# Bringing the first pair's keys and queries in as 256-byte rows and turning them on TensorE

## The chip, the cores and the metric

The kernel runs on one core of one Trainium2 chip. The metric is the device time of one execution in microseconds (us), lower is better. Durations of single instructions are given in us or ns from one profiled execution. The engines are TensorE (PE, its weight loads are listed apart as PEld), VectorE (DVE), ScalarE (ACT), GpSimd (POOL) and SyncE (SP), which here only issues transfers; ACT issues a few as well.

## The reference, cut to what matters

Attention with a threshold, and then a feed-forward block with ELU on its output:

```python
# q, k, v: (8, 8, 576, 64) fp32; tau: a scalar; w_in: (512, 2048), w_out: (2048, 512)
scores = (1 / sqrt(64)) * q @ k.transpose(0, 1, 3, 2)
thresh = max(scores, axis=-1) - tau
scores = where(scores >= thresh, scores, -1e9)
attn = exp(scores - max(scores, axis=-1))
attn = attn / (sum(attn, axis=-1) + 1e-9)
x = (attn @ v).transpose(0, 2, 1, 3).reshape(4608, 512)
h = x @ w_in
g = where(h > 0, h, exp(min(h, 0)) - 1)
out = g @ w_out
```

## The kernel before, in words

The 64 heads are worked in 32 pairs, two heads of one batch side by side: head 0 of a pair in partitions 0 to 63, head 1 in 64 to 127. Of the 576 positions of a head, 512 (MAIN, NC = 4 blocks of P = 128) make full steps, and the last 64 (TAIL) of both heads make a fifth step. A step is a tile of 128 queries against all 576 keys of both heads: scores on TensorE (`scores`, L673), the maximum on VectorE (`max_of`, L730), threshold or pivot (`bound_of`, `pivot_of`), exponential on ScalarE, mask and sum, normalisation, a turn of the weights (L792 with copies at L808, in the opening) and the product with the values (L925, L930). When the first batches are done, the feed-forward matmuls are woven in, and from then on TensorE works on them between the steps.

The scores need queries and keys with the 64 numbers of a head along the partitions, `qT` of 128 x 576 and `kT` of 128 x (64 + 576). In memory a position is a row of 64 fp32 numbers, 256 bytes. `load` brings a pair in so that VectorE's transpose, which turns blocks of 32 x 32, gives the wanted layout: every row is cut into two pieces of 32 numbers (128 bytes), which go to different groups of 32 partitions, one DMA for each group. `prep_q` and `prep_k` are those transposes. In `kT` the first 64 columns hold, for head 1, a copy of the last 64 keys (`copy_k`, on GpSimd), so that both heads can use halves of 288 keys that start at different columns. For pair 0 `prep_q` turns the first 256 queries alone; the rest follow later (`load_rest_of_q`, `rest_of_q`).

The order of the instructions is written out by hand: `manual_schedule`, with tasks that have a time of their own (`task`, sorted at the end of `early_tasks`) and a table of offsets, MOVED. Each engine runs its instructions in that order and waits where the data isn't there. The first task is `start`, which loads pair 0, keeps TensorE busy with 22 transposes of the identity (`idle(22)`), turns queries and keys, and works out from tau the constants of the thresholds (`read_tau`, six small VectorE instructions, L435 to L440). The tasks after it load pair 1 (which takes over the buffers `qm` and `km` of pair 0), the values, and the rest of the queries. Step 0 works head by head (HEADS_APART): all scores of head 0, then those of head 1.

Matmul outputs lie in PSUM. Up to step LATE there are two pools: `psum["t"]` with two buffers for turns and value products, and `psum["s"]` with three buffers of two banks for scores. `room_for` keeps the handed-out order of the first.

The Exp of `keep` in `start` loads ScalarE's table ahead of its first use.

Of the kernel before, what the change touches and what calls it, by code (L numbers as in the profile page):

```python
# [10 lines left out]
FP32 = mybir.dt.float32  # L11
# [357 lines left out]
def kernel(  # L369
# [10 lines left out]
    nc = tc.nc  # L380
    PSUM = bass.MemoryType.PSUM
    P = 128
    B, H, S, D = q.shape
    DM, DF = moe_w_in.shape
    NC = S // P
    MAIN = NC * P
    TAIL = S - MAIN
    HALF = S // 2
    T = 32
    NT = P // T  # L390
# [11 lines left out]
    const = ctx.enter_context(tc.tile_pool(name="const", bufs=1))  # L402
# [7 lines left out]
    raw = attention.enter_context(tc.tile_pool(name="raw", bufs=1, side="right"))  # L410
# [6 lines left out]
    wstage = early.enter_context(tc.tile_pool(name="wstage", bufs=2))  # L417
    wpool = [wstage]
    banks = ExitStack()
    psum = {"t": banks.enter_context(tc.tile_pool(name="ps_t", bufs=2, space=PSUM))}  # L420

    first = ExitStack()
    psum["s"] = first.enter_context(tc.tile_pool(name="ps_s0", bufs=3, space=PSUM))

    ident = wstage.tile([P, P], FP32, name="ident", bufs=1)
    make_identity(nc, ident)
    idents = [ident]
# [2 lines left out]
    tau_sb = const.tile([P, 1], FP32, name="tau_sb")  # L430
# [15 lines left out]
    def w_in_at(j, f, n):  # L446
        return w_in_sb[f // QF][:, j, f % QF : f % QF + n]
# [4 lines left out]

    xtail = dram.tile([KJ, P, B * TAIL], FP32, name="xtail", bufs=1)

    NQD, NVD = 2, 2
    qds = [const.tile([P, P], FP32, name=f"qd{i}") for i in range(NQD)]
    vds = [const.tile([P, P], FP32, name=f"vd{i}") for i in range(NVD)]
    vds_first = [wstage.tile([P, P], FP32, name=f"vf{i}", bufs=1) for i in range(NVD)]
    for t in qds + vds_first + vds:
        nc.gpsimd.memset(t, 0.0)  # L460


# [1 line left out]
    pieces = [(moe_w_in, w_in_at(j, n, WN), j, n) for n in range(0, DF, WN) for j in range(KJ)]  # L464
# [56 lines left out]
    raws, pairs, firsts = {}, {}, {}  # L521


    def load(pr, parts=("qm", "km", "v"), shared=False, queue=nc.sync, pieces=tuple((i, d) for i in range(2) for d in range(2)),
             js=slice(0, S // T)):
        b, j = divmod(pr, NPAIR)
        tiles = raws.setdefault(pr, {})
        for name, src in (("qm", q), ("km", k), ("qr", q)):
            if name not in parts:
                continue  # L530
            if name not in tiles:
                tiles[name] = raw.tile([P, S // T, T], FP32, name="qm" if shared else name)
            m = tiles[name]
            if pr in QK_PE:
                if "ends" not in tiles:
                    tiles["ends"] = wstage.tile([TAIL, 2, 2, D], FP32, name="ends", bufs=1)
                both, blocks = src[b, 2 * j : 2 * j + 2], blocks_of(pr, name[0])
                for i in range(2):
                    queue.dma_start(blocks[:, :, i], both[i, :MAIN].rearrange("(c p) d -> p c d", p=P))
                queue.dma_start(tiles["ends"][:, int(name == "km")], both[:, MAIN:].rearrange("i p d -> p i d"))  # L540
                continue
            for i, d in pieces:
                r = (2 * i + d) * T
                queue.dma_start(
                    m[r : r + T, js if name != "qr" else slice(0, S // T - js.start)],
                    src[b, 2 * j + i].rearrange("(j t) d -> t j d", t=T)[:, js, d * T : (d + 1) * T],
                )
        if "v" in parts:
            load_v(pr)
# [12 lines left out]
    def room_q(pr):  # L562
        if pr < 2:
            both = wstage.tile([P, 2 * S + TAIL], FP32, name="x", bufs=2)
            qT, firsts[pr] = both[:, :S], both[:, S:]
        else:
            qT = qkp.tile([P, S], FP32, name="qT")
        pairs[pr] = [qT, None, qds[pr % NQD]]
        return qT

    def room_k(pr):
        kT = pairs[pr][1] = firsts[pr] if pr < 2 else qkp.tile([P, TAIL + S], FP32, name="kT")
        return kT

    def prep_q(pr):
        qT, n = room_q(pr), S if pr else 2 * P
        nc.vector.transpose(qT[:, :n], raws[pr]["qm"].rearrange("p j d -> p (j d)")[:, :n])
# [8 lines left out]
    def prep_k(pr):  # L586
        kT = room_k(pr)
        km = raws[pr]["km"].rearrange("p j d -> p (j d)")
        for c0, c1 in ((0, HALF), (HALF, S)) if pr == 0 else ((0, S),):
            nc.vector.transpose(kT[:, TAIL + c0 : TAIL + c1], km[:, c0:c1])  # L590


    def blocks_of(pr, name):
        return raws[pr][name + "m"].rearrange("p j d -> p (j d)")[:, :MAIN].rearrange("p (c i d) -> p c i d", i=2, c=NC)
# [32 lines left out]
    def copy_k(pr):  # L627
        kT = pairs[pr][1]
        nc.gpsimd.tensor_copy(kT[D:, :TAIL], kT[D:, S:])
# [18 lines left out]
    def vectors(pr):  # L648
        st = {x: small.tile([P, 2], FP32, name=x) for x in ("mx", "th", "su", "rs")}
        if not pr:  # L650
            st["nb"] = wstage.tile([P, 2], FP32, name="nb", bufs=4)
        step_no[0] += 1
        st["sm"] = totals[:, step_no[0] % 6]
        return st


    def scores(pr, i, hs):
        qT, kT, qd = pairs[pr]
        if hs[0] == 0:
            open_steps[pr, i] = vectors(pr)  # L660
        st = open_steps[pr, i]
        if "f" in psum and not apart:
            both = psum["s"].tile([P, 2, 2, 512], FP32, name="sc")
            scs = {h: both[:, h] for h in hs}
        else:
            scs = {h: psum["s"].tile([P, 2, 512], FP32, name="sc") for h in hs}
        halves = [(a, h) for a in range(2) for h in hs]
        if (pr, i) in HEADS_APART:
            halves.sort(key=lambda x: x[1])
        for a, h in halves:  # L670
            k0 = a * HALF + (0 if h else TAIL)
            r, qs = (slice(h * D, (h + 1) * D), qT[:, i * P : (i + 1) * P]) if i < NC else (slice(0, P), qd)
            nc.tensor.matmul(scs[h][:, a, :HALF], qs[r], kT[r, k0 : k0 + HALF], start=True, stop=True)  # L673
        if len(hs) == 2 and "f" in psum and not apart:
            st["both"] = both
        for h in hs:
            st[h] = scs[h]
# [617 lines left out]
    def task(x, t, key, f, *needed):  # L1295
        each = "_".join(map(str, x)) if isinstance(x, tuple) else x
        made[x] = [t + (MOVED.get(key, 0.0) if key else 0.0) + MOVED.get(each, 0.0), len(made), f, needed, False]
# [10 lines left out]
    def early_tasks():  # L1308
# [10 lines left out]
        def idle(n):  # L1319
            room_for("t", lambda: None)  # L1320
            rt = psum["t"].tile([P, NC, P], FP32, name="rt", tag="rt")
            for _ in range(n):
                transpose(rt[:, 0], ident)

        def start():
            load(0, ("qm",), js=slice(0, 2 * NT))
            load(0, ("km",), queue=nc.scalar, pieces=((0, 0), (0, 1), (1, 0)))
            load(0, ("km",), pieces=((1, 1),))
            nc.scalar.activation(keep, keep, AF.Exp)
            nc.sync.dma_start(tau_sb, tau.to_broadcast([P, 1]))  # L1330
            idle(22)
            prep_q(0)
            prep_k(0)
            read_tau()
            copy_k(0)

        def load_rest_of_q():
            raws[0]["qr"] = wstage.tile([P, S // T - 2 * NT, T], FP32, name="qr", bufs=1)
# [32 lines left out]
        turned = {}  # L1371
        for pr in range(1, NPAIR + 6):
            old = ("sc", number[pr - 2, NC]) if pr > 1 else None
            own = pr < NPAIR
            for x, name in enumerate("qk"):
                n = 2 * pr - 2 + x if own else number[pr - 1, 2 + x]
                k, late_ = kind(n), n >= LATE
# [30 lines left out]
            for x, name in enumerate("qk"):  # L1408
                n = 2 * pr - 1 + x if own else number[pr - 1, 3 + x]
                late_ = n >= LATE  # L1410
                task(("load", name, pr + 1), begin[n] + (7.0 if late_ else -1.0 if own else 4.6), f"l{name}{kind(n)}",
                     lambda pr=pr, name=name: load(pr + 1, (name + "m",)), ("prep", name, pr), ("last", pr) if pr in QK_PE else None)
            if pr > 1:
                n = 2 * pr - 3 if own else number[pr - 1, 3]
# [5 lines left out]
        for i, (n, x) in enumerate(slots):  # L1420
            late_, k, t = n >= LATE, f"{kind(n)}{x}", begin[n]
# [43 lines left out]
        for u in range(NU):  # L1465
            n = 26 + 3 * u // 2 if u < NU - 2 else SWITCH + u - NU + 2
# [3 lines left out]
        for n in range(MIDDLE):  # L1470
            pr, i = steps[n]
# [4 lines left out]
            t, k, hs, late_ = begin[n], kind(n), heads_of(i), n >= LATE  # L1476
# [3 lines left out]
            if n == LATE:  # L1480
                task("switch", t, None, switch, *rooms)
            rooms += [("exp" if (n, h) in MASK_ACT else "mask", n, h) for h in hs]
            at_ = (lambda a, b, c=0: t + c) if last_ else (lambda a, b, c=0: t + b) if late_ else (lambda a, b, c=0: t + a)
            task(("sc", n), t + 0.2 if late_ else t - 2.6 if i in (2, NC) else t - 2.0, f"sc{k}", lambda pr=pr, i=i, hs=hs: scores(pr, i, hs), ("prep", "q", pr),
                 ("prep", "k", pr), ("scale", pr) if pr else None, ("copy", "k", pr), ("copy", "q", pr) if i == NC else None,
                 ("sc", n - 1) if n else None, "rest" if (pr, i) == (0, 2) else None, *two)
            for h in hs:
# [127 lines left out]
    with tc.manual_schedule():  # L1615
# [31 lines left out]
        ends = []  # L1647
# [226 lines left out]
        queue = deque()  # L1874
# [212 lines left out]
        for pr in range(JOINED, NP + 2):  # L2087
            t = clock[0]
            b = pr // NPAIR
# [93 lines left out]
        for f in range(EARLY_IN + 1, NFT):  # L2183
            t = max(begin + 0.4 + 2.73 * (f - EARLY_IN), start_of[g7, f] - LEAD)
# [78 lines left out]
        for f in range(NFT):  # L2263
            split_weights(begin + 22.0 + 3.9 * f if f < OUT_EARLY else start_f(middle, f) - 9.0, ("out", f), w_out_of(f),
                          lambda f=f: out_done(f))
            for g, t0 in ((g7, middle), (g8, end)):
                t = start_f(t0, f) - (11.5 if f < EDGE else 6.0) + 3.2 * f * (f < EDGE)
# [84 lines left out]
```

## Time and profile before

| what | value |
|---|---|
| median of 3 runs | 1259.23 us (1258.12 to 1259.68) |
| the profiled execution | 1259.32 us |
| its span, first to last instruction | 1257.5 us |
| PE busy in 0 to 32 us, 32 to 64 us, 64 to 96 us | 27.20, 30.20, 32.00 us |
| first score instruction on PE | 6.23 us |
| DMA busy share in 0 to 32 us, mean rate | 0.71, 136 GB/s |

The profile is of one execution. The share of busy time is an average over stages with different limits, so the opening has to be read by itself, instruction by instruction. A line of the timeline gives the start, the length, the engine, the line of the kernel, the operation, what it writes and reads, the shape, how many instructions were merged into it, and in brackets how long the engine had been idle and what ended the wait. "L792 PE MATMUL rt<-ident" is a transpose on TensorE. A matmul's listed length contains its way through the array, so instructions overlap and the pace of a run is its length, less one tail, by their number.

### The profile page before, as it was taken

How to read it: one execution, taken by the hardware profiler on the slowest of the kernel's cores; microseconds unless marked ns; L12 is line 12 of the kernel's file. 1: busy time of each engine (PE TensorE's matmuls, PEld its weight loads, DVE VectorE, ACT ScalarE, POOL GpSimd, SP SyncE). 2: the span in 40 equal slices, each digit the busy share in tenths (PEclk: the TensorE clock that was granted, in tenths of full speed). 3: DMA queues.
4: the chain of work that ended last, by engine and by line, in shares of the span. 5: the costliest groups of instructions: out<-in, count | busy, mean ns of one | idle time of the engine just before them, and what ended most of it. 6: DMA issues, size and time to landing. Idle time of an engine off the chain costs nothing.

```text
span 1257.5 us, 21116 instructions
## 1 busy us (share of the span) xinstructions
PE 1243.9 (99%) x6598; PEld 957.0 (76%) x6598; DVE 1040.3 (83%) x2199; ACT 635.2 (51%) x1331; POOL 727.1 (58%) x1061
## 2 busy tenths in 40 slices
PE   8999999999999999999999999999999999999998
PEld 6676576467878787888778787878788887788886
DVE  7888778789798988898889879898889876776983
ACT  7989776664352526253534435252625353465330
POOL 4778655687475847666576747584766655122000
PEclk9999999999999999999999999999999999999999
DMA  7557688998889898998989998999889885000001
GB/s 134 151 177 177 177 244 234 260 248 216 239 239 266 245 240 224 241 263 228 252 206 253 237 231 231 256 257 240 228 238 262 221 241 175 20 1 1 1 34 34
DMA packets 325551, 245.74 MB, mean 195 GB/s; under 512 B 209216, under 2 KB 289984, under 8 KB 325440
## 3 DMA queue, kind: packets, MB, share of 16 engines
q1 hardware_dynamic: 323264, 243.65, 72.2%
q8 instruction: 52, 0.85, 0.3%
q10 hardware_dynamic: 2176, 0.75, 0.2%
q14 instruction: 59, 0.48, 0.1%
HBM read 154.53 MB, written 89.78 MB: 194 GB/s over the span
## 4 chain that ended last, share of the span: by engine, by line
PE 90%; DVE 3%; DMA 2%; ACT 2%; issue 1%; SPq 1%; POOL 1%; DVEq 0%; ACTq 0%; POOLq 0%
PE f L1678 23%; PE f L1818 22%; PE sc L977 8%; PE sc L1050 7%; PE f L2278 7%; PE f L2203 5%; PE f L1102 4%; PE sc L673 3%; PE f L1154 3%; PE f L2216 2%; PE pv L930 2%; PE rt L792 1%; PE sc L1042 1%; PE sc L1037 1%; DMA there<-x 1%
## 5 line engine op out<-in xcount | busy, mean ns | idle before, releaser
L984 DVE TENSOR_REDUCE mx<-sc 128x1 f32<-128x576 f32 x207 | 148.3, 750 | 28.5 <-PE sc L977 24.6
L726 POOL TENSOR_SCALAR w<-w,rs 128x576 f32<-128x576 f32 x144 | 115.8, 813 | 70.0 <-DVE rs L789 69.8
L1004 ACT ACTIVATE w<-sc,mx 128x576 f32<-128x576 f32 x113 | 81.5, 740 | 116.0 <-DVE mx L984 98.7
L868 DVE STREAM_TRANSPOSE x<-w 128x512 f32<-128x512 f32 (+1 forms) x153 | 108.9, 744 | 15.3 <-POOL w L726 11.3
L996 POOL TENSOR_SCALAR th<-mx,ntau 128x2 f32<-128x2 f32 (+1 forms) x114 | 33.8, 297 | 133.3 <-DVE mx L984 133.3
L977 PE MATMUL sc<-kT,qT 64*128 64x448 f32 (+4 forms) x736 | 103.4, 416 | 0.2 <-ACT xs L1066 0.2
L977 PEld LDWEIGHTS sc<-kT,qT 64*128 64x128 f32 x736 | 81.0, 186 | 25.1 <-issue 16.5
L1011 DVE SCALAR_TENSOR_TENSOR w<-sc,th,w 128x576 f32<-128x576 f32 x113 | 88.2, 811 | 9.4 <-ACT w L1004 9.2
L1678 PE MATMUL f<-xt,sw 128*128 128x256 f32 x384 | 93.8, 386 | 1.8 <-DVE g L1700 1.8
L1678 PE MATMUL f<-xt,w_in 128*128 128x256 f32 x384 | 92.2, 382 | 0.0
L1818 PE MATMUL f<-w_out,s 128*128 128x256 f32 x384 | 92.0, 382 | 0.1
L1818 PE MATMUL f<-w_out,g 128*128 128x256 f32 x384 | 92.0, 382 | 0.0
L1678 PE MATMUL f<-x,w_in 128*128 128x256 f32 x384 | 90.9, 379 | 0.0
L1818 PE MATMUL f<-t,s 128*128 128x256 f32 x384 | 90.8, 379 | 0.0
L726 POOL TENSOR_SCALAR e<-e,rs 128x576 f32<-128x576 f32 x91 | 67.1, 741 | 35.6 <-DVE rs L789 34.2
L1678 PEld LDWEIGHTS f<-xt,sw 128*128 128x128 f32 x384 | 69.4, 189 | 18.6 <-issue 4.8
L1678 PEld LDWEIGHTS f<-xt,w_in 128*128 128x128 f32 x384 | 71.7, 190 | 12.7 <-ACT w L1692 2.2
L1818 PEld LDWEIGHTS f<-w_out,g 128*128 128x128 f32 x384 | 72.0, 190 | 12.4 <-issue 3.1
L1818 PEld LDWEIGHTS f<-w_out,s 128*128 128x128 f32 x384 | 71.9, 190 | 12.4 <-issue 2.5
L1678 PEld LDWEIGHTS f<-x,w_in 128*128 128x128 f32 x384 | 72.8, 190 | 10.5 <-ACT s L1692 0.6
L1818 PEld LDWEIGHTS f<-t,s 128*128 128x128 f32 x384 | 72.8, 190 | 10.3 <-POOL s L1765 0.4
L1765 POOL TENSOR_TENSOR s<-g 128x256 f32<-128x256 f32 x96 | 74.9, 785 | 7.9 <-DVE g L1728 7.5
(316 smaller groups left out, 3103.5 us busy)
## 6 DMA issues: line engine op xcount, KB each, us to landing
there<-x SPq DMA_DIRECT2D x444, 144.0 KB, 3.5
wTb<-there SPq DMA_DIRECT2D x58, 576.0 KB, 6.5
wTa<-there SPq DMA_DIRECT2D x53, 576.0 KB, 5.0
sw<-win_sums SPq DMA_DIRECT2D x46, 384.0 KB, 4.9
t<-wout_sums SPq DMA_DIRECT2D x33, 512.0 KB, 6.2
qm<-in_q_dram SPq DMA_DIRECT2D x124, 72.0 KB, 4.9
wst<-in_moe_w_in_dram SPq DMA_DIRECT2D x16, 512.0 KB, 4.4
vm<-in_v_dram SPq DMA_DIRECT2D x64, 128.0 KB, 3.9
```

The costliest lines, as they stand in the source:

```text
L726: nc.gpsimd.tensor_scalar(wv, wv, st["rs"][:, h : h + 1], 1.0, ALU.mult, ALU.mult)
L868: nc.vector.transpose(x[:, :, c0 : c0 + nc_], src.rearrange("p (c g n) -> p g c n", c=nc_, n=T))
L977: on_banks(nc.tensor.matmul(o, qT[r, i * P : (i + 1) * P], kT[r, k0 : k0 + n], start=True, stop=True, skip_group_check=True), o)
L984: on_banks(nc.vector.tensor_reduce(st["mx"][:, h : h + 1], st["sc", h], axis=AX.XY if i == NC else AX.X, op=ALU.max, negate=True), st["sc" ...
L1004: on_banks(nc.scalar.activation(st["e", h], st["sc", h], AF.Exp, bias=st["mx"][:, h : h + 1]), st["sc", h])
L1011: on_banks(nc.vector.scalar_tensor_tensor(st["e", h], st["sc", h], st["th"][:, h : h + 1], st["e", h], ALU.is_ge, ALU.mult, accum_out=st[" ...
L1050: on_banks(nc.tensor.matmul(o, vm[:, h, c], parts[part][:, g0:g1, h * (NC + 1) + c], start=False, stop=(c == NC - 1), skip_group_check=Tru ...
L1678: nc.tensor.matmul(loc["banks"][place], left[:, j], right[:, j], start=(begins and j == 0), stop=(j == 1), skip_group_check=True)
L1765: engine.tensor_tensor(o, x, y, op)
L1818: nc.tensor.matmul(place(m), lhs, rhs, start=(begins and v == 0), stop=(v == RU - 1), skip_group_check=True)
L2203: nc.tensor.matmul(o, w.rearrange("p (j f) -> p j f", j=KJ)[:, j], m, start=(j == 0 and x == 0), stop=(j == KJ - 1 and x == 1), skip_group ...
L2278: nc.tensor.matmul(banks8[2 * i + x // 2], h[:, tok], w, start=(f == 0 and x != 1), stop=(f == NFT - 1 and x != 0), skip_group_check=True)
```

## The change

Pair 0 is no longer loaded in pieces of 128 bytes. The first 128 queries, each of the four blocks of 128 keys, and the last 64 keys of both heads come as rows of 256 bytes, one DMA each with positions along the partitions, on SP's and ACT's queues in turn; the second 128 queries follow behind tau. TensorE turns each block by a transposing matmul with the identity into PSUM, and VectorE and ScalarE copy the results to `qT` and `kT`. The copy of the last keys for head 1, done by GpSimd before, is made by VectorE from PSUM. PSUM rooms for the turns are both buffers of the pool "t" and all three of the pool "s". In place of the 22 transposes of the identity TensorE is given ten fp32 matmuls of a blank tile (128 x 64 outputs), and one more of them between the turns. The blank tile is `qds[0]`, which VectorE now sets to zero ahead of everything else, where GpSimd set it before. The second 128 queries are turned and copied (by ScalarE) behind the scores of step 0. The rest of pair 0's queries and all other pairs are loaded and turned as before. The buffer `qm` is first used by pair 1.

```diff
+    NQD, NVD = 2, 2
+    qds = [const.tile([P, P], FP32, name=f"qd{i}") for i in range(NQD)]
+    nc.vector.memset(qds[0], 0.0)
     ident = wstage.tile([P, P], FP32, name="ident", bufs=1)
     make_identity(nc, ident)
...
-    for t in qds + vds_first + vds:
+    for t in qds[1:] + vds_first + vds:
         nc.gpsimd.memset(t, 0.0)
...
+    def first_rows(name, c, n=P):
+        return {"q": q, "k": k}[name][0, :2, c * P : c * P + n].rearrange("i p d -> p i d")
...
         def start():
-            load(0, ("qm",), js=slice(0, 2 * NT))
-            load(0, ("km",), queue=nc.scalar, pieces=((0, 0), (0, 1), (1, 0)))
-            load(0, ("km",), pieces=((1, 1),))
+            tiles = raws[0] = {"km": raw.tile([P, S // T, T], FP32, name="km")}
+            kb = blocks_of(0, "k")
+            qb = wstage.tile([P, 2, 2, D], FP32, name="qb", bufs=1)
+            ends = tiles["ends"] = wstage.tile([TAIL, 2, D], FP32, name="ends", bufs=1)
+
+            nc.sync.dma_start(qb[:, 0], first_rows("q", 0))
+            nc.scalar.dma_start(kb[:, 0], first_rows("k", 0))
+            nc.sync.dma_start(kb[:, 1], first_rows("k", 1))
+            nc.scalar.dma_start(kb[:, 2], first_rows("k", 2))
+            nc.sync.dma_start(kb[:, 3], first_rows("k", 3))
+            nc.scalar.dma_start(ends, first_rows("k", NC, TAIL))
+            nc.sync.dma_start(tau_sb, tau.to_broadcast([P, 1]))
+            nc.sync.dma_start(qb[:, 1], first_rows("q", 1))
             nc.scalar.activation(keep, keep, AF.Exp)
-            nc.sync.dma_start(tau_sb, tau.to_broadcast([P, 1]))
-            idle(22)
-            prep_q(0)
-            prep_k(0)
+            blank, turned = (psum["t"].tile([P, NC, P], FP32, name="rt", tag="rt") for _ in range(2))
+            a, b, c = (psum["s"].tile([P, 2, 512], FP32, name="sc") for _ in range(3))
+            qT, kT = room_q(0), room_k(0)
+
+            def warm(n):
+                for _ in range(n):
+                    nc.tensor.matmul(blank[:, 0, :TAIL], qds[0], qds[0][:, :TAIL], start=True, stop=True)
+
+            def turn_rows(dst, src, n=P):
+                nc.tensor.matmul(dst, src.rearrange("p i d -> p (i d)"), ident[:n, :n], is_transpose=True, skip_group_check=True)
+
+            warm(10)
+            turn_rows(turned[:, 0], qb[:, 0])
+            nc.vector.tensor_copy(qT[:, :P], turned[:, 0])
+            warm(1)
+            turn_rows(a[:, 0, :P], kb[:, 0])
+            warm(1)
+            turn_rows(a[:, 0, P : 2 * P], kb[:, 1])
+            nc.vector.tensor_copy(kT[:, TAIL : TAIL + 2 * P], a[:, 0, : 2 * P])
+            warm(1)
+            turn_rows(b[:, 0, :P], kb[:, 2])
+            nc.scalar.copy(kT[:, TAIL + 2 * P : TAIL + 3 * P], b[:, 0, :P])
+            warm(1)
+            turn_rows(c[:, 0, :P], kb[:, 3])
+            nc.scalar.copy(kT[:, TAIL + 3 * P : S], c[:, 0, :P])
+            turn_rows(turned[:, 1, :TAIL], ends, TAIL)
+            nc.vector.tensor_copy(kT[:, S:], turned[:, 1, :TAIL])
+            nc.vector.tensor_copy(kT[D:, :TAIL], turned[D:, 1, :TAIL])
+
+            def rest_of_first_q():
+                rt = psum["t"].tile([P, NC, P], FP32, name="rt", tag="rt")
+                turn_rows(rt[:, 0], qb[:, 1])
+                nc.scalar.copy(qT[:, P : 2 * P], rt[:, 0])
+
+            first_q.append(rest_of_first_q)
             read_tau()
-            copy_k(0)
...
-                 lambda pr=pr, i=i, hs=hs: scores(pr, i, hs), ("prep", "q", pr),
+                 lambda pr=pr, i=i, hs=hs: (scores(pr, i, hs), first_q and first_q.pop()()), ("prep", "q", pr),
```

More of the change, by code (lines that the diff above doesn't have):

```diff
@@ L453 @@
     xtail = dram.tile([KJ, P, B * TAIL], FP32, name="xtail", bufs=1)
-    NQD, NVD = 2, 2
-    qds = [const.tile([P, P], FP32, name=f"qd{i}") for i in range(NQD)]
     vds = [const.tile([P, P], FP32, name=f"vd{i}") for i in range(NVD)]
     vds_first = [wstage.tile([P, P], FP32, name=f"vf{i}", bufs=1) for i in range(NVD)]
-    for t in qds + vds_first + vds:
+    for t in qds[1:] + vds_first + vds:
         nc.gpsimd.memset(t, 0.0)
@@ L1323, in idle @@
                 transpose(rt[:, 0], ident)
+        first_q = []
         def start():
-            load(0, ("qm",), js=slice(0, 2 * NT))
-            load(0, ("km",), queue=nc.scalar, pieces=((0, 0), (0, 1), (1, 0)))
-            load(0, ("km",), pieces=((1, 1),))
-            nc.scalar.activation(keep, keep, AF.Exp)
-            nc.sync.dma_start(tau_sb, tau.to_broadcast([P, 1]))
-            idle(22)
-            prep_q(0)
-            prep_k(0)
+            tiles = raws[0] = {"km": raw.tile([P, S // T, T], FP32, name="km")}
[10 more added lines that the diff above has]
+            nc.sync.dma_start(qb[:, 1], first_rows("q", 1))
+            nc.scalar.activation(keep, keep, AF.Exp)
+            blank, turned = (psum["t"].tile([P, NC, P], FP32, name="rt", tag="rt") for _ in range(2))
[28 more added lines that the diff above has]
+            first_q.append(rest_of_first_q)
@@ L1483, in early_tasks @@
             at_ = (lambda a, b, c=0: t + c) if last_ else (lambda a, b, c=0: t + b) if late_ else (lambda a, b, c=0: t + a)
-            task(("sc", n), t + 0.2 if late_ else t - 2.6 if i in (2, NC) else t - 2.0, f"sc{k}", lambda pr=pr, i=i, hs=hs: scores(pr, i, hs), ("prep", "q", pr),
+            task(("sc", n), t + 0.2 if late_ else t - 2.6 if i in (2, NC) else t - 2.0, f"sc{k}", lambda pr=pr, i=i, hs=hs: (scores(pr, i, hs), first_q and first_q.pop()()), ("prep", "q", pr),
                  ("prep", "k", pr), ("scale", pr) if pr else None, ("copy", "k", pr), ("copy", "q", pr) if i == NC else None,
```

## The prediction, made before the change was run

> **What bounds the kernel now.** I read the page's span and busy shares first, then the chain of waits in order of time, then the timeline of the first 16 us.
>
> ```profile
> span 1257.5 us, 21116 instructions
> PE 1243.9 (99%) x6598; PEld 957.0 (76%) x6598; DVE 1040.3 (83%) x2199; ACT 635.2 (51%) x1331; POOL 727.1 (58%) x1061
> ```
>
> TensorE is the bound over the whole. The stages of 32 us show where it is not: PE is busy 27.20 of the first 32 us and 30.20 of the next, and 32.00 of 32 in nearly every later one. So from about 64 us on the end is a fixed amount of matmul work; what the opening saves or loses moves everything after it, and only the opening has slack. PE idles 6.6 us in it.
>
> ```profile
> 0.73 2.73 DMA km<-in_k_dram
> 3.47 2.28 DMA tau_sb<-in_tau_dram
> 5.75 0.44 DVE x L590
> 6.23 1.25 PE sc L673 x4
> 7.50 0.77 DVE mx L730
> ```
>
> The chain of waits (start, length, what) begins with the loads of pair 0, goes over the VectorE turns of the keys and the scores of the first head to the first maximum at 7.50 us. I use that maximum as the milestone: what moves it moves the rest.
>
> ```profile
> 0.72 1.88 SPq L544 DMA_DIRECT2D qm<-in_q_dram  x4
> 0.73 1.53 ACTq L544 DMA_DIRECT2D km<-in_k_dram  x3
> 1.48 4.66 PE L792 MATMUL rt<-ident 128*128 128x128 f32 x22 [1.48 <-POOL ident masks.py:199]
> 2.65 0.45 SPq L544 DMA_DIRECT2D km<-in_k_dram  x1
> 5.37 0.44 DVE L577 STREAM_TRANSPOSE x<-qm 128x256 f32<-128x256 f32 x1 [5.37 <-DMA qm<-in_q_dram]
> 6.46 0.11 DVE L435 TENSOR_SCALAR pos<-tau_sb 128x1 f32<-128x1 f32 x1
> 10.72 1.97 PE L792 MATMUL rt<-ident 128*128 128x128 f32 x16
> 17.14 0.29 DVE L808 COPY wTa<-rt 128x128 f32<-128x128 f32 x1
> 28.71 0.27 ACT L808 COPY wTb<-rt 128x128 f32<-128x128 f32 x1 [0.35 <-PE rt L792]
> 53.75 1.89 PE L1102 MATMUL f<-xt,w_in 128*128 128x256 f32 x8
> ```
>
> In the timeline the reader is to see that VectorE sits until 5.37 for the queries, that the last of these was issued at about 2.13 and the last keys at 2.65 (landing 2.8 us later, by the DMA view), and that PE is filled meanwhile with 22 idle transposes.
>
> **Loads.** Before: 4 issues of queries and 4 of keys, 416 KB in 3328 pieces of 128 B. After, ahead of the first scores: one of queries, four of keys, one of ends, 352 KB in 1408 rows of 256 B. The DMA view of 2.2 to 2.6 us (all 128 B) and of 33 to 34 us (nearly all 256 B):
>
> ```profile
> DMA packets 624, 0.08 MB, mean 192 GB/s; under 512 B 624, under 2 KB 624, under 8 KB 624
> DMA packets 989, 0.25 MB, mean 255 GB/s; under 512 B 986, under 2 KB 986, under 8 KB 988
> ```
>
> Transfer falls from 416/192 = 2.2 us to 352/255 = 1.4 us. Issues: SP takes 1.88/4 = 0.47 each and ACT 0.51, so the third of each queue starts at 1.66 and 1.75 instead of a fifth on SP at 2.65. Loads of the opening landed 1.9 to 3.3 us after issue; I take 2.3 because less is queued. So queries and first keys are there at 3.0, the last keys and ends at 4.0 (bounds 3.6 and 5.05). tau is SP's fourth issue, 2.13, and lands at 4.6 by its own 2.5. The second 128 queries are SP's fifth, and there by 5.1, before they are used.
>
> **Queues that move.** Pair 1's queries waited for pair 0's queries in the same buffer (issue at 5.85) and its keys followed at 7.90. After, the queries have another buffer and can go once a first load has landed, about 3; the keys still wait, now for PE's turns of the keys. SP's queue behind them (first weights at 9.98, values at 10.53) comes up to 2.7 us earlier. No engine waits for a DMA from 8 to 120 us, so I cost this at nothing; the cover is those loads' lead. If it went, pair 1's turns at 12.47 would be late next. ACT's queue keeps three issues, so its table load stays at 2.29.
>
> **PE before the data.** The first blank tile is now set by VectorE (0.20 by POOL's row for it), so fillers start at about 1.0 instead of 1.48. warm(10) is ten fp32 matmuls, two instructions each (the scores show 12 for 6): 20, with 128 stationary and 64 moving columns. No row has this form. Every pace I can read follows the moving columns: 8 of 256 take (1.89-0.38)/7 = 216 ns each, 16 transposes of 128 take (1.97-0.27)/15 = 113. The 22 transposes at the start are at half pace, 213 each, until about 5.4, as their lengths show (the half-microsecond at 4.5, then at 6):
>
> ```profile
> L792 PE MATMUL rt<-ident 128*128 128x128 f32 x5 | 1.3, 421 | 0.0
> L792 PE MATMUL rt<-ident 128*128 128x128 f32 x2 | 0.4, 273 | 0.0
> ```
>
> The granted clock reads 1.00 throughout and does not show that. Low end: 64 moving columns at half pace, 107 ns, 20 take 2.1 us, done at 3.1. High end: the weight load paces, at 213 ns, 4.3 us, done at 5.3. A load's time does grow with its columns:
>
> ```profile
> L1678 PEld LDWEIGHTS f<-x,w_in 128*128 128x128 f32 x384 | 72.8, 190 | 10.5 <-ACT s L1692 0.6
> L1050 PEld LDWEIGHTS sc<-wTa,vm 128*64 128x64 f32 x368 | 26.4, 137 | 15.8
> ```
>
> 53 ns for 64 columns, so some 107 for 128 at full pace. I take 107 at half pace too, since no row shows a load setting the pace. The Trainium skill ("TensorE: Matmul & The Clock Gate", LDWEIGHTS) gives columns divided by 1.2, 107 ns for 128; it agrees with 2 x 53 here, and by it warm(10) is 2.1 us, an estimate. The same page (Part 4: PE-mode transpose) says transposes do not bring the clock up; the trace disagrees, 421 to 273 ns with only transposes running.
>
> **Turns and copies.** PE then runs six turns and four warm(1), in order: at half pace a turn 0.21, a warm(1) 0.21. From 3.1: queries done 3.4, first keys 3.8, second 4.2, third 4.65, fourth 5.1, ends 5.2 (64 rows), each with some 0.2 of tail. Copies by the rows of 0.27 and 0.29 (0.36 for 256 columns): VectorE has the first two blocks by 4.8, ACT the third by 5.1 and the fourth by 5.6, VectorE the ends by 5.65 and the second copy (POOL's 0.23 before) by 5.9. Scores of the first head can start at 5.2 and end between 6.3 (full pace) and 6.8. Behind the copies on VectorE stand the six tau instructions, 6.46 to 7.46 before, 1.0 us: 5.9 to 6.9. So the first maximum comes at 6.95, **0.55 earlier**; VectorE, not PE, is last there. At full pace all through, with the short landing, it would be 5.65 (gain 1.9, tau then last); with the loads' high end some 0.5 later than before.
>
> **The wait added.** Scores of the second step need ACT's copy of the second queries: both heads' scores to 7.3, turn 7.5, copy 7.85, next scores 7.9 to 9.15; the maximum there is ready at 9.2, where VectorE is free at 8.9: 0.3 late. Behind the copy on ACT is the first sink (8.67 before), which needs its threshold at 8.0, so it is not held. The fourth maximum, which waited for PSUM (10.83), comes at 10.35: the 0.3 is swallowed and 0.5 is kept. SyncE, GpSimd and the later order are as they were.
>
> **Sum:** 1259.32 us in the profiled execution (span 1257.5) less 0.5 is 1258.8; the runs' median is 0.09 lower, so 1258.7.
>
> **Rivals.**
> *The filler is paced by weight loads.* Done at 5.3; then 14 instructions (six turns, eight halves of filler) at 0.107 reach 6.8, copies 7.3, tau 8.3, maximum 8.35: 0.85 later, 1260.1. For: 190 against 137 ns. Against: 216 ns for 256 columns shows loads hidden behind matmuls. The Trainium skill (same page, Part 3, what overlaps) says that loads overlap only with matmuls of other row groups; by that 20 x (107 + 107) gives the same 4.3 us, but the trace's 216 for full-height matmuls is against it.
>
> *The clock stays low (slower).* The filler fills the array half as much and PE waits for loads from 3.1 to 4; if the rate has not doubled when the scores begin, PE's gaps at 8.4 to 9.6 keep it down until the dense stretch from 16 us. Price: first head's scores 1.25 to 2.5 eats the 0.5; the 16 idle transposes at 10.72 take 1.7 longer and hold the turns at 13.43; the next scores on the chain (14.87) lose 1.25: with the rest about 3.3 us, 1262.5. It decides once the scores' pace is still half after 9 us. Against: here the rate rose 3.9 us after PE began, and now PE begins 0.5 sooner.
>
> *More than the start.* All favourable ends, 1.9, and 0.7 of the opening's 6.6 us of PE idle closing because loads come 2.7 us sooner: 1256.6. Against: no wait for a DMA in that stretch.
>
> *Hidden anyway.* The gain is used up by the weights' conversion at 51 to 62 us, which stands in the chain on POOL and VectorE: 1259.2. Against: it too is ordered behind the opening.
>
> **Chances.** Forecast 0.38, filler paced by loads 0.18, hidden 0.04: together 0.60 for within 0.2% (2.5 us, about what a measurement of this kernel can tell from no change). Clock low 0.24: slower. More than the start 0.16: faster. The range goes from 1256.8, the 1.9 gain and 0.6 of spread in the runs, to 1262.4; about half of each outer case lies outside. The forecast's own range is 1257.4 to 1259.8.
>
> **What would show it.** Right: filler of about 2.1 us, last keys landing near 4.0, last VectorE copy near 5.9, first maximum near 6.95, and the same 0.5 us at 64 us. Filler ending past 5 shows the second case; score instructions still at half pace near 9 us the third. I am wrong if the landing is not shorter, if the half pace lasts, or if the shift at 64 us differs from that of the first maximum.

## The result, and the profile after

The changed kernel took 1261.86 us (median of 11 runs, 1261.2 to 1262.89) against 1259.18 us before (11 runs): a ratio of 1.0026, 95% interval 1.0018 to 1.0034. It is slower by 2.7 us, where 0.5 us less was forecast. That lies inside the wide range that was given (1256.8 to 1262.4), but outside the forecast's own (1257.4 to 1259.8) and near the case of the low clock (1262.5). Its profiled execution took 1262.17 us with a span of 1260.4.

The page of the changed kernel:

```profile
span 1260.4 us, 21140 instructions
PE 1249.4 (99%) x6611; PEld 961.7 (76%) x6611; DVE 1040.6 (83%) x2201; ACT 636.0 (50%) x1334; POOL 728.4 (58%) x1059
```

PE is busy 5.5 us longer (1243.9 before), although it has only 13 instructions more: some of them take longer. Where, the chain of waits of its opening says (start, length, what):

```profile
1.04 4.53 PE rt L1352 x20
5.57 0.21 PE rt L1355
5.78 0.32 PE rt L1352 x2
...
7.91 0.30 PE rt L1355
8.21 2.86 PE sc L677 x8
11.07 0.42 PE rt L1355
11.51 0.28 ACT x L1378
11.83 3.02 PE sc L677 x8
14.85 4.17 PE rt L796 x24
19.02 1.18 PE sc L677 x7
```

Before, this chain began with loads, ran over VectorE and reached the scores at 6.23. Now it is TensorE from 1.04 us on: first the filler (L1352), then turns with a filler between each two, then scores. No load stands in it. The timeline of the same execution gives the single steps:

```profile
1.03 4.34 PEld L1352 LDWEIGHTS rt<-qd 128*128 128x128 f32 x20 [1.03 <-DVE qd L427]
1.04 4.53 PE L1352 MATMUL rt<-qd 128*128 128x64 f32 x20 [1.04 <-DVE qd L427]
5.82 0.29 DVE L1359 COPY x<-rt 128x128 f32<-128x128 f32 x1 [4.83 <-PE rt L1355]
8.01 3.06 PE L677 MATMUL sc<-x 64*128 64x288 f32 x8
9.66 0.15 DVE L443 TENSOR_SCALAR ntau<-ntau 128x1 f32<-128x1 f32 x1
10.27 0.76 DVE L734 TENSOR_REDUCE mx<-sc 128x1 f32<-128x576 f32 x1 [0.46 <-PE sc L677]
14.78 3.36 PE L796 MATMUL rt<-ident 128*128 128x128 f32 x16
```

The 20 filler instructions take 4.5 us, one weight load of about 215 ns behind the other (the loads end at 5.4); the first queries, issued at 0.72, had landed after 2.2 us, the keys by about 4.2 and the ends at 4.9 (DMA view). VectorE waits 4.83 us for PE, no longer for a load. The first maximum comes at 10.27 instead of 7.50, and VectorE waits 0.46 us for the scores before it, with the tau instructions done. And the 16 idle transposes, 1.97 us before, take 3.36: TensorE is still at half pace at 15 us, and the eight scores at 8.01 take 3.06. The lengths of single transposes show when that ends (windows of half a microsecond, at 16.5 and at 18; last number: mean ns of one):

```profile
L796 PE MATMUL rt<-ident 128*128 128x128 f32 x5 | 1.3, 421 | 0.0
L796 PE MATMUL rt<-ident,w 128*128 128x128 f32 x5 | 0.7, 273 | 0.0
```

Before, the same instruction had gone from 421 to 273 ns between 5 and 6 us. The row of granted clock reads 1.00 in both kernels.

The first value product starts at 23.56 us (19.59 before), and the feed-forward lines keep that shift of about 4.0 us up to the first matmul of x with w_in (271.2 against 267.2). After a stretch in which the DMA engines are busy 0.94 of the time it is 2.9 us (303.4 against 300.5 for the first with w_out), and so at the end.

### The profile page after: what moved, and what is told of

Same layout as the page of the kernel before. It is cut to its first block, busy times and chain, and to the rows that moved or that the text cites. A ratio compares the mean times of both kernels' runs of the same rounds, so it can differ in the third digit from the quotient of the medians.

```text
span 1260.4 us, 21140 instructions
## 1 busy us (share of the span) xinstructions
PE 1249.4 (99%) x6611; PEld 961.7 (76%) x6611; DVE 1040.6 (83%) x2201; ACT 636.0 (50%) x1334; POOL 728.4 (58%) x1059
## 4 chain that ended last, share of the span: by engine, by line
PE 92%; DVE 2%; DMA 2%; ACT 1%; SPq 1%; issue 1%; POOL 0%; DVEq 0%; ACTq 0%; POOLq 0%
PE f L1864 23%; PE f L1724 22%; PE sc L981 8%; PE sc L1054 7%; PE f L2324 7%; PE f L2249 5%; PE f L1106 4%; PE sc L677 4%; PE f L1158 3%; PE f L2262 2%; PE pv L934 2%; PE rt L796 2%; PE sc L1046 1%; DMA there<-x 1%; PE sc L1041 1%; DVE x L872 1%
## 5 line engine op out<-in xcount | busy, mean ns | idle before, releaser
L981 PEld LDWEIGHTS sc<-kT,qT 64*128 64x128 f32 x736 | 80.7, 186 | 25.3 <-issue 16.5
```

Of the source, the lines that this page charges most:

```text
L981: on_banks(nc.tensor.matmul(o, qT[r, i * P : (i + 1) * P], kT[r, k0 : k0 + n], start=True, stop=True, skip_group_check=True), o)
```

## The experiments

Each set of experiments was timed beside the kernel before: 1258.56 us (median of 29 runs) in the first set and 1258.58 us (27 runs) in the second. The ratios below are to these, not to 1259.18.

The theory after this result: TensorE's pace doubles only after a stretch in which columns stream through it nearly all the time. The filler moves 64 columns behind a weight load of 128, so it streams half of the time; the pace stays halved until the 16 idle transposes. The rivals: zeros don't count as work; or the turns with their waits keep the pace down, whatever fills the gaps.

**wide_filler**: 128 columns moved instead of 64.

```diff
-                    nc.tensor.matmul(blank[:, 0, :TAIL], qds[0], qds[0][:, :TAIL], start=True, stop=True)
+                    nc.tensor.matmul(blank[:, 0], qds[0], qds[0], start=True, stop=True)
```

> Only change to the changed kernel: the filler matmuls move 128 columns of the blank tile instead of 64. If weight loads pace the filler (214 ns each at half pace in the changed kernel's profile), its length stays 4.3 to 4.5 us. Theory fill (TensorE's pace doubles only after a stretch in which columns stream nearly all the time; 64 columns behind a load of 128 fill half of it): the pace doubles near 5 us, the turns then take about 1.5 instead of 2.8 us, the first maximum comes near 8.0 instead of 10.27, the 16 idle transposes take 2.0 instead of 3.4, and the time falls by 3 us or more below the changed kernel's, to about 1258.5 to 1260. Rival data (an all-zero tile does not count as work): stays at half pace to 17 us, time unchanged, 1262. Rival turns (the waiting turns and gaps keep the pace down whatever fills): unchanged too.

1259.64 us, ratio to the kernel before 1.001 (1.0001 to 1.0019). The timeline of its PE:

```profile
1.04 3.89 PE L1352 MATMUL rt<-qd 128*128 128x128 f32 x20 [1.04 <-DVE qd L427]
4.76 0.27 PE L1355 MATMUL rt<-ident,qb 128*128 128x128 f32 x1
6.41 1.97 PE L677 MATMUL sc<-x 64*128 64x288 f32 x8
11.36 1.97 PE L796 MATMUL rt<-ident 128*128 128x128 f32 x16
```

Twice the columns take less time, 3.89 us instead of 4.53, since the pace doubled before the filler's end, at about 4.0 (in a second profile, below, it did not, and the 20 took 4.63; so 64 columns cost as much as 128 at half pace: it was the weight loads, of 128 columns in both, that paced the narrow filler). The first turn has a length of 0.27 instead of 0.42, the eight score instructions 1.97 instead of 3.06, the idle transposes 1.97 again. First maximum 8.20. Its median is 2.2 us below the change's, where 3 or more was expected. Neither rival leaves room for this: the tile is still zero, and the turns are the same.

**ones_filler**: 64 columns, of ones.

```diff
+    ones = w_in_sb[0][:, 0, :P]
+    nc.vector.memset(ones, 1.0)
...
-                    nc.tensor.matmul(blank[:, 0, :TAIL], qds[0], qds[0][:, :TAIL], start=True, stop=True)
+                    nc.tensor.matmul(blank[:, 0, :TAIL], ones, ones[:, :TAIL], start=True, stop=True)
```

> Only change to the changed kernel: the filler multiplies a tile of ones instead of zeros, still 64 columns. Theory fill: nothing changes, half pace to about 17 us, 1261.5 to 1262.5. Rival data: the pace doubles near 5 us and the time falls to about 1259.

1262.15 us, 1.0031 (1.0019 to 1.0042). First maximum 10.41, half pace to about 17.4 us (17.6 in the change): zeros or ones make no difference.

**no_filler**: all filler matmuls left out.

```diff
             def warm(n):
-                for _ in range(n):
-                    nc.tensor.matmul(blank[:, 0, :TAIL], qds[0], qds[0][:, :TAIL], start=True, stop=True)
+                return
```

> The changed kernel with all its filler matmuls taken out. The data land at 3.1 to 4.9 us, so the turns run at half pace from 3.2, the last copy ends near 5.6, the tau instructions near 6.6, the first maximum comes near 7.0 to 7.4. Theory fill: the pace still doubles only in the dense stretch after 11 us, so of the 2.8 us won at the first maximum most is kept: 1259 to 1260. Rival: if the 64-column filler did help to raise the pace a little sooner, less than 1.5 us is won, 1260.5 or more.

1260.16 us, 1.0012 (1.0003 to 1.0021). The filler of the change is worse than none: 1.7 us were won, a little less than expected. Its PE:

```profile
3.08 0.45 PE L1354 MATMUL rt<-ident,qb 128*128 128x128 f32 x1 [3.08 <-DMA qb<-in_q_dram]
5.22 0.34 PE L1354 MATMUL rt<-ident,ends 64*128 64x64 f32 x1 [0.48 <-DMA ends<-in_k_dram]
5.35 3.13 PE L677 MATMUL sc<-x 64*128 64x288 f32 x8
12.19 2.55 PE L796 MATMUL rt<-ident 128*128 128x128 f32 x16
```

Here the loads are what PE waits for (3.08 and 5.22), the row loads seen undisturbed; the last one lands about 0.3 us sooner than the last keys before. The scores still run at half pace, the first maximum is at 7.63, and the pace doubles within the idle transposes, at about 13.3.

**before_half_filler**: the kernel before, with 22 instructions of fp32 matmuls of 64 columns for its 22 transposes.

```diff
-            idle(22)
+            room_for("t", lambda: None)
+            rt = psum["t"].tile([P, NC, P], FP32, name="rt", tag="rt")
+            for _ in range(11):
+                nc.tensor.matmul(rt[:, 0, :TAIL], ident, ident[:, :TAIL], start=True, stop=True)
```

> The kernel before with one change: its 22 idle transposes replaced by 22 instructions of fp32 matmuls of the identity with 64 moving columns. Loads and VectorE turns stay as they were. Theory fill: the pace stays halved past 10 us, the first maximum comes near 8.8 instead of 7.50 (scores of one head 1.25 us longer), the 16 idle transposes take 3.4 us, and the time rises by 2.5 to 4 us, 1261.7 to 1263. Rival turns (it is the new way of turning that keeps the pace down): no change, 1259.2.

1261.03 us, 1.0017 (1.0008 to 1.0026): a little less than expected, but most of the loss, without any of the new loads or turns.

```profile
1.48 4.96 PE L1334 MATMUL rt<-ident 128*128 128x64 f32 x22 [1.48 <-POOL ident masks.py:199]
12.96 3.67 PE L792 MATMUL rt<-ident 128*128 128x128 f32 x16
```

First maximum 8.69, the idle transposes 3.67 us (1.97 in the kernel before), the first value product at 22.73. Half pace lasts to about 17.9 us. By itself it costs 3.1 us there, of the change's 4.0, and the turns on TensorE are not needed for it.

**wide_short, wide_tau, short_tau, filler96.** The second set asks whether the rest of the plan holds once the filler streams. wide_short is wide_filler (128 columns) with half of the filler ahead of the turns:

```diff
-            warm(10)
+            warm(5)
```

> Filler of 128 columns as in wide_filler, but warm(5) instead of warm(10) ahead of the first turn, so that PE is free for the turns at about 3.2, when the first queries and keys have landed. Theory fill: what counts is that columns stream without a break, turns and filler alike, so the pace still doubles near 4.5 to 5; turns end near 5.5, VectorE's copies near 6, tau near 7.1, first maximum near 7.2 (8.20 in wide_filler, 7.50 before). Time about 1 us below wide_filler, 1258.5 to 1259. Rival: the pause between filler and turns costs the doubling; then scores at half pace and first maximum near 8, time 1260 or more as without filler.

1259.23 us, 1.0004 (0.9995 to 1.0013): no difference from the kernel before that can be told, where 1258.5 to 1259 was expected. Its profile is nearly the one that was forecast for the change, with the filler done at 3.3, turns to 5.3 and the first maximum at 7.08 (6.95 forecast); the fourth comes at 10.33 (10.35 forecast, 10.83 before); its span is 1256.9, 0.6 below before.

wide_tau is wide_filler with tau first:

```diff
+            nc.sync.dma_start(tau_sb, tau.to_broadcast([P, 1]))
             nc.sync.dma_start(qb[:, 0], first_rows("q", 0))
...
+            read_tau()
             nc.vector.tensor_copy(qT[:, :P], turned[:, 0])
```

> wide_filler with tau issued first on SP and its six VectorE instructions ahead of the copies, where VectorE is idle. If these 1.0 us on VectorE are what stands between the last copy and the first maximum, it comes near 7.6 instead of 8.20 (now bound by the scores' end) and the time falls by about 0.6 us, to 1259.0. If scores were last anyway, the first maximum stays at 8.2 and the time at 1259.6.

1258.98 us, 1.0003 (0.9994 to 1.0012). Its first maximum came at 8.76, not 7.6: the pace doubled at about 6.0 instead of 4.0, and the scores were last. The moment of doubling had moved by more than tau was worth, so the place of tau is left open. The time is the one that was expected if tau counted, but by another way, and so is no evidence for it.

> Both together: warm(5) of 128 columns and tau first. First maximum near 6.5 to 6.9, 0.6 to 1.0 us sooner than before the change; time 0.5 to 0.9 us below the kernel before, if the opening's shift is kept; equal to it if the stretch from 256 to 300 us, which gave back 1 us of the 4 us loss, also takes 1 us of a gain.

The edits of wide_short and wide_tau together: 1259.4 us, 1.0008 (0.9999 to 1.0017), first maximum 8.11. With tau issued first the queries landed later, PE stood still for 0.50 us at 4.04, and the pace doubled at about 6.2. A miss: no gain.

```diff
-                    nc.tensor.matmul(blank[:, 0, :TAIL], qds[0], qds[0][:, :TAIL], start=True, stop=True)
+                    nc.tensor.matmul(blank[:, 0, :96], qds[0], qds[0][:, :96], start=True, stop=True)
```

> The changed kernel with filler of 96 columns: columns stream for 160 of each 214 ns. If the rate needs nearly full streaming, half pace lasts to about 17 us as with 64; if three quarters are enough, it doubles near 5 us as with 128, and the first maximum comes near 8.2 instead of 10.27.

filler96 is the change with 96 columns. One run: the 20 instructions take 4.58 us, so the load paces here too; the pace doubles at about 7.2, the first maximum is at 9.64, the idle transposes take 1.97. This is neither of the two expected cases: three quarters are enough, at least in this execution, but late.

**The moment of doubling.** It differed between kernels with the same filler, so four kernels were profiled once more.

> The kernel before once more, for a second profile. If the moment at which PE's pace doubles is set by the program alone, it comes at about 5.4 us again. If it hangs on a window that runs free of the program, it comes somewhere from 4.3 to 8 us, and the first maximum moves from 7.50 by up to 1.3 us.

The 22 transposes took 4.96 instead of 4.66 us, first maximum 7.70: the doubling came at about 6.5 instead of 5.7.

> The changed kernel once more, for a second profile. Theory fill: half pace past 12 us here too, since no stretch before 11.8 streams without a break for long, so the first maximum comes near 10.3 again; with a free-running window the doubling may move from 17.5 to anywhere between 14 and 18 us.

As in its first profile: maximum 10.27, 16 transposes in 3.22 us, doubling at about 17.4.

> wide_short once more. Its first profile had the doubling at 3.8 us, 2.8 us after PE began, the soonest of all. Set by the program: 3.8 again, first maximum 7.08. Free-running: later, up to 7 us, first maximum 7.1 to 8.5, which would explain that its median is not below that of the kernel before although this profile is.

Its PE, first the profile before, then this one:

```profile
3.93 0.27 PE L1355 MATMUL sc<-ident,km 128*128 128x128 f32 x1
5.19 0.24 PE L1355 MATMUL rt<-ident,ends 64*128 64x64 f32 x1
5.32 1.93 PE L677 MATMUL sc<-x 64*128 64x288 f32 x8
```

```profile
3.97 0.42 PE L1355 MATMUL sc<-ident,km 128*128 128x128 f32 x1
5.89 0.42 PE L1355 MATMUL sc<-ident,km 128*128 128x128 f32 x1
6.25 0.37 PE L1355 MATMUL rt<-ident,ends 64*128 64x64 f32 x1
6.41 2.02 PE L677 MATMUL sc<-x 64*128 64x288 f32 x8
```

The same program: a turn at 3.9 us is fast (0.27) in one execution, and one at 5.9 still slow (0.42) in the other. The turn of the ends at 6.25 is slow too (0.37 against 0.24), and the first score, from 6.41, takes 724 ns against 477 in the first profile and 791 in the change. So the doubling lies at 3.8 and at about 6.8, the first maximum at 7.08 and 8.25.

> wide_filler once more. Its first profile had the doubling at 4.5 us. Set by the program: 4.5 again, first maximum 8.20. Free-running: 4 to 7 us, first maximum 8.0 to 9.3 (wide_tau, with the same filler, had 5.9 and 8.76).

```profile
1.04 4.63 PE L1352 MATMUL rt<-qd 128*128 128x128 f32 x20 [1.04 <-DVE qd L427]
```

Doubling at about 7.0 instead of 4.0 (4.5, in the expectation, was read more coarsely), the 20 filler instructions in 4.63 us, first maximum 9.66 instead of 8.20.

All of them, with the two times of a kernel profiled twice:

| kernel | first maximum, us | first value product, us | median, us | ratio to before in its set |
|---|---|---|---|---|
| before | 7.50, 7.70 | 19.59, 19.77 | 1259.18 | 1 |
| the change | 10.27, 10.27 | 23.56, 23.42 | 1261.86 | 1.0026 |
| ones_filler | 10.41 | 23.52 | 1262.15 | 1.0031 |
| before_half_filler | 8.69 | 22.73 | 1261.03 | 1.0017 |
| no_filler | 7.63 | 20.77 | 1260.16 | 1.0012 |
| wide_filler | 8.20, 9.66 | 20.23, 21.70 | 1259.64 | 1.001 |
| wide_short | 7.08, 8.25 | 19.09, 20.27 | 1259.23 | 1.0004 |
| wide_tau | 8.76 | 20.78 | 1258.98 | 1.0003 |
| short_tau | 8.11 | 20.12 | 1259.4 | 1.0008 |
| filler96 | 9.64 | 21.67 | 1261.43 (one run) | none |

The times follow the first value product rather than the first maximum, if only roughly (no_filler and wide_tau have the same one): what counts is also how long the half pace lasts behind the maximum. In the change the shift grows from 2.8 us at the first maximum to 4.0 at the first value product.

## Why the prediction was wrong

**Where it failed: the pace of the filler, and with it the clock.** The first step is the price of the filler. "I take 107 at half pace too, since no row shows a load setting the pace." That no row showed it was because no instruction of the kernel before moves fewer columns than its load brings. The load took 215 ns, the end of the range that I had put beside it, so the filler ended at 5.4 and not at 3.1, and each warm(1) between the turns took 0.32 and not 0.21 (chain of waits). The rows of 190 and 137 ns, from which I had worked out 107 ns of load at full pace, were the better neighbour: at half pace they double like the matmuls. The Trainium skill's columns divided by 1.2 ("TensorE: Matmul & The Clock Gate", LDWEIGHTS), 107 ns for 128, fits the fp32 loads at full pace and not at half. Its Part 3, which speaks of no overlap, gave the right 4.3 us for a reason that wide_filler's second profile refutes: all at half pace, 20 with 128 columns take 4.63 us and 20 with 64 take 4.53.

**The clock.** This is the step that cost most: before_half_filler, which delays no turn, has 3.1 of the 4.0 us at the first value product. The forecast took the doubling near 5 us for granted (before the change it was at about 5.7, by quarters of a microsecond, not 5.4), and held the low clock for a rival at 0.24. It came as that rival said: scores at half pace, and the idle transposes of 3.4 us instead of 2.0, which pushed the later turns. Its condition, half pace after 9 us, was met. Its reason, half as much streaming, is borne out by wide_filler, which changes the columns alone; the pause between filler and loads that it also named didn't exist, since the filler outlasted the loads. It priced the loss at 3.3 us against 2.7 measured. wide_filler, whose filler takes 3.89 or 4.63 us against 4.53 in the change, loses about 2 us less than the change (1.001 against 1.0026). Two rivals came true at once, and I had given them as alternatives although a filler paced by loads is exactly one that streams little: the second followed from the first. The copy of the second queries on ScalarE (11.51) stands in the chain, too, and the next scores wait 0.36 us for it; the forecast had counted on that wait being hidden.

**What held, and what else did not.** The issues: the third ones at 1.72 and 1.79 (1.66 and 1.75 forecast). The queries and the first keys, there at 2.9 and 3.1 (3.0 forecast), and the last keys, near 4.2 (4.0 forecast). The ends were late: 4.9 by the DMA view, and in no_filler PE waits for them until 5.22, where 4.0 had been forecast with a bound of 5.05. Tau landed 2.9 us after its issue at 2.23. The queries of pair 1 were issued at 3.30 instead of 5.85, but what stands behind them on SP came no earlier (first weights at 9.93, 9.98 before), since the keys of pair 1 waited for the late turns. The copies are 0.23 to 0.29 as priced, that of 256 columns 0.42 for 0.36. Of the 0.55 us at the first maximum, wide_short showed 0.42 in its better execution (7.08 against 7.50), and all of the 0.5 at the fourth. That kernel is the nearest to a filler as I had priced it, and its time can't be told from that of the kernel before.

**The opening moves everything after it** is right to about 1 us. The shift was 4.0 at 267 us and 2.9 at 300 in the first two profiles, and 3.6 and 4.1 in the second two. That stretch took 33.3 us in one execution of the kernel before and 31.3 in the other (267.2 to 300.5, and 267.4 to 298.7), so how much of the loss it gives back is left open.

No version that was run is shown to beat the kernel before. Where the filler streams, the intervals leave the row loads and TensorE turns a gain of at most 0.8 us (wide_tau, 0.9994), less than the moment of doubling moves the first maximum by itself.

## What to carry to other kernels

Idle matmuls that are to bring TensorE to full pace should move as many columns as their weight load brings; a narrow filler costs as much time and may raise the pace late (96 of 128, in one run) or not at all (64). Before pricing a new instruction shape by a rule that all rows obey, ask whether any row could have broken it. And a start that is tuned to the doubling of the pace is tuned to something that moves by up to 3 us from one execution to the next.

## What the runs showed of the hardware

- With 64 columns moved behind each fp32 load of 128, TensorE stayed at half pace for 16 us, in the change through filler, turns and two runs of scores of 3 us each (four profiles of three kernels); with 128 it doubled 2.8 to 6.0 us after its first instruction, over eight profiles (the two with 22 idle transposes included); with 96 at 6.2 us, in one. Ones or zeros made no difference.
- The moment differs between executions of one program: 3.8 and 6.8, 4.0 and 7.0 us. The Trainium skill ("TensorE: Matmul & The Clock Gate", Part 1) tells of a window of 3.4 us that runs free of the kernel; a spread of 3.0 us fits that but doesn't show it, and the 2.8 us of wide_short from PE's first instruction to the doubling are less than the window. The page gives 4 us with half a microsecond either way; here it was wider.
- Transposes alone brought the pace up: in the kernel before, where nothing else had run on TensorE, at 5.7 us. The same page (Part 4: PE-mode transpose) says they do not; here the measurement decides.
- The granted clock in the profile's rows read 1.00 (0.999 in some) throughout; half pace is seen only in the lengths, 421 against 273 ns for a transpose of 128 x 128 in fp32.
- Scores that use 64 of the array's 128 rows ran for 3 us at half pace without bringing the pace up (no_filler, 5.35 to 8.48, and again from 9.23); it rose 1.1 us into the transposes of full height behind the second run. Whether that is for their height or for the moment was not tried.
